# Block-causal attention with a gated convolution: the products of P and V in tiles of 64x64 instead of 64x32

## The chip, the cores and the metric

The kernel runs on one core of a Trainium2 chip. The metric is the device time of one execution in microseconds, the median of three runs. The matrix engine is called PE here (its weight loads PEld), the vector engine DVE, the scalar engine ACT, GpSimd POOL, and the engine that issues DMAs SP.

## The reference

Eight batches, eight heads, 576 positions, 64 channels a head. Attention is causal by blocks of 64 positions, and its output, heads side by side, goes through a layer with a convolution over positions and a gate:

```python
B, H, S, D = 8, 8, 576, 64
scores = matmul(q, k.transpose) / sqrt(D)
scores = where(block_i >= block_j, scores, -1e9)        # blocks of 64 positions
attn = exp(scores - max); attn = attn / (sum + 1e-9)
x = matmul(attn, v)                                     # then (B, S, H*D) = (8, 576, 512)
h = maximum(x @ w_in, 0)                                # w_in 512 x 1024
conv_out[s] = sum_k conv_w[k] * h[s + k - 1]            # three taps
out = (h * sigmoid(conv_out)) @ w_out                   # w_out 1024 x 512
```

## The kernel before

Work goes by pairs of heads: 32 pairs, four to a batch. The first batch's pairs are done in two parts, A (positions 0 to 255, blocks 0 to 3) and B (blocks 4 to 8); the 28 other pairs are done whole (blocks 0 to 8). Behind the last pair of a batch come its dense projections, `ffn` (L1005: x times w_in; L1071: the gated result times w_out), in float32r, with tiles of 128x128.

For a pair, `stage_s` makes the scores on PE (L862), in up to three sets of blocks: (8, 5), (7, 6) and (4, 3, 2, 1, 0). Each call takes 64 rows of the array (one head's 64 channels) and 32 columns (32 query positions): a tile of 64x32. DVE takes the maximum (L874), ACT the exponential with its sum (L890). `inverse` makes 1/sum on POOL and DVE, spread over a tile `rb`. `stage_pv` then

- transposes P in 32x32 pieces on DVE into `ptw` (or `pta` for part A), L939;
- multiplies by V on PE, L952, in `mm`. For each block u of keys it makes eight calls: y (two halves of the 64 channels), g (two halves of the 64 key and query rows) and h (two heads). V is the stationary operand, 64 rows by 32 columns; P moves, 32 query positions for every block that sees u, so 288 columns for u = 0 of a whole pair and 32 for u = 8. The results accumulate over u in two banks of PSUM, at partitions 64h + 32y, in bank g;
- multiplies the sum by `rb` on DVE (L963), rounds the high part on ACT (L967) and leaves the rest to POOL, for the projections.

A whole pair's P·V step has 9 x 8 = 72 calls. The step of part B has as many, with 160 columns for u = 0 to 4; that of part A has 4 x 8.

The order is written out by hand: the numbers in `ORDER` (L19) say in which sequence `Plan.follow` emits the operations recorded by `pl.op`, `BANKS` which PSUM bank each takes, and `FILLS` where spare matmuls stand (L1166). The durations given to `pl.op` do not set the order. One operation of the plan is one whole step of P·V; its calls stand one behind the other on PE.

Of the kernel before, what the change touches and what calls it, by code (L numbers as in the profile page):

```python
# [331 lines left out]
def kernel(  # L332
# [10 lines left out]
    nc = tc.nc  # L343
# [54 lines left out]
    def bank(tag):  # L398
        return pl.bank(psum, tag)

    def both(pair):
        a, b = sorted(x.slot for x in pair)
        assert b == a + 1
        return banks[:, a:b + 1]
# [35 lines left out]
    def held(tag, t, cap, before=None):  # L440
        b = Bin([])
        b.t = t[len(pl.tags.setdefault(tag, [])) % cap]
        hist = pl.tags[tag]
        hist.append(b)
        if len(hist) > cap:
            b.before = hist[-1 - cap]
        elif before is not None:
            b.before = before
        return b
# [14 lines left out]
    def c_act(n, psum=True, ap=False, acc=False):  # L464
        return (0.051 if psum else 0.093) + n / 1200.0 + (0.093 if ap else 0) + (0.08 if acc else 0)

    def c_dve(n, fast=False, two_in=False):
        return 0.065 + n / (1920.0 if fast else 960.0) + (0.05 if two_in else 0.0)

    def c_pool(n, two_in=False):  # L470
        return 0.145 + n * 0.0022 if two_in else 0.16 + n / 1200.0
# [348 lines left out]
    def c_tile(widths, more, least):  # L820
        return sum(max(2 * 0.000836 * w + more, least) for w in widths)
# [104 lines left out]
    def stage_pv(pq, done, vs, xx, at, part, ready):  # L926
        vat, vbufs, vdone = vs
        done, (rb, inv) = done
        b0, b1 = SPAN[part]
        if part == "A":  # L930
            pt = held("pta", pta, 2)
            rise, sl = 3, 0
        else:
            pt = held("ptw", [ptw], 1, firstp)
            rise, sl = RISE, 0
        ps = []
        for b, ns, t0 in done:
            def tr(b=b, x=pq[b], pt=pt):
                nc.vector.transpose(pt.ap[:, :, b:b + rise * b + 1:rise, :], x.ap.rearrange("p h (u n) -> p h u n", n=32))  # L939

            ps.append(pl.op(DVE, c_dve(64 * (b + 1)) + 0.025, tr, t0, deps=ns, bufs=[pq[b], pt] + ([firstp] if part == "A" else [])))
        vb = [bank("v"), bank("v")]

        def mm():
            for u in range(b1):
                lo = max(u, b0)
                for y in range(2):
                    for g in range(2):
                        for h in range(2):
                            r = slice(64 * g, 64 * g + 64)  # L950
                            o = 64 * h + 32 * y
                            nc.tensor.matmul(both(vb)[o:o + 32, g, 32 * (lo - b0):32 * (b1 - b0)].rearrange("p (b n) -> p b n", n=32),  # L952
                                             vat(u, h)[r, 32 * y:32 * y + 32], pt.ap[r, h, rise * u + lo:rise * u + b1, :],
                                             start=(u == 0), stop=(u == b1 - 1), skip_group_check=True)

        o = pl.op(PE, c_tile([32 * (b1 - max(u, b0)) for u in range(b1)], 0.03, 0.15), mm, at, deps=ps + vdone, bufs=vb + vbufs + [pt], area=0.85, rows64=3)
        w = 32 * (b1 - b0)

        def out(j):
            return xx[j].ap[:, 64 * b0:64 * b1].rearrange("p (b g n) -> p g b n", g=2, n=32)  # L960

        def mul():
            nc.vector.tensor_tensor(out=rb.ap[:, :, 0:b1 - b0, :], in0=both(vb)[:, :, 0:w].rearrange("p g (b n) -> p g b n", n=32),  # L963
                                    in1=rb.ap[:, :, 0:b1 - b0, :], op=ALU.mult)

        def evh():
            nc.scalar.activation(out=out(0), in_=rb.ap[:, :, 0:b1 - b0, :], func=AF.Copy)  # L967

        def evl():
            eng = nc.gpsimd if LOWPOOL else nc.vector  # L970
            eng.tensor_tensor(out=out(1), in0=rb.ap[:, :, 0:b1 - b0, :], in1=out(0), op=ALU.subtract)

        e = pl.op(DVE, c_dve(2 * w), mul, at + 3.0, deps=[o, inv], bufs=vb + [rb])
        e = pl.op(ACT, c_act(2 * w, False), evh, at + 3.5, deps=[e], bufs=[xx[0], rb])
        if LOWPOOL:
            es = [pl.op(POOL, c_pool(2 * w, True), evl, at + 4.0, deps=[e], bufs=[xx[0], xx[1], rb])]
        else:
            es = [pl.op(DVE, c_dve(2 * w, two_in=True), evl, at + 4.0, deps=[e], bufs=[xx[0], xx[1], rb])]
        ready(es)
# [141 lines left out]
    for i, (p, part) in enumerate(visits):  # L1121
        opv, ot = offs[part]
        b0 = base[i]
# [78 lines left out]
```

## Time and profile before

| what | value |
|---|---|
| time, median of 3 runs | 702.47 us (700.16 to 703.66) |
| the profiled execution: its time, its span | 701.78 us, 699.8 us |
| mean granted clock of PE | 0.995 of 2.4 GHz |
| PE, PEld busy | 665.2 us, 556.9 us |
| DVE, ACT, POOL busy | 574.9, 535.2, 325.3 us |
| L952 (P·V), PE busy | 93.0 us in the steps with `ptw` |
| L862 (scores), PE busy | 106.2 us |

The span runs from the first to the last instruction of the program. The chain of waits goes back from the last instruction to what released it, or to the instruction before on the same engine; "issue" in it, and as a releaser, is time in which the engine waited for nothing that the profile shows. A matmul's recorded duration holds its way through the array, so matmuls that follow each other overlap, and the steps between their starts say more than the durations.

### The profile page before, as it was taken

To read this page: it belongs to the slowest core of one execution; us is meant where nothing else is said; L and a number is where in the kernel's file an instruction comes from. 1 tells how busy PE (TensorE), PEld (TensorE's weight loads), DVE (VectorE), ACT (ScalarE), POOL (GpSimd) and SP (SyncE) were. 2 spreads that over 40 slices of the span, in tenths; PEclk is the share of its full clock that TensorE was granted. 3 is DMA by queue.
4 is the path that set the end of the run, shared out by engine and by line. 5 is a ranking of instruction groups with operands and counts; after the bars stand their busy time and mean duration, and the time that the engine had idled before them with its cause. 6 is when DMAs were issued, how large, how long until landed. Compare 5 with 4: busy or idle time off the path is not lost.

```text
span 699.8 us, 29716 instructions
## 1 busy us (share of the span) xinstructions
PE 665.2 (95%) x12059; PEld 556.9 (80%) x12059; DVE 574.9 (82%) x1345; ACT 535.2 (76%) x2000; POOL 325.3 (46%) x730
## 2 busy tenths in 40 slices
PE   9879989999999899999999999999999999999997
PEld 7556768878888688788888788787979787889986
DVE  4989989988997679897988779897989978986562
ACT  5877879967978667796988678977887768875663
POOL 2664545645545325436344444555436424444341
PEclk9999999999999999999999999999999999999999
DMA  7986653445255441416343443343343424130001
GB/s 169 213 175 132 127 114 50 94 95 88 46 108 92 78 86 39 81 42 128 76 78 68 84 99 59 61 105 58 73 95 62 93 64 96 27 68 1 35 27 61
DMA packets 238541, 58.58 MB, mean 84 GB/s; under 512 B 228524, under 2 KB 232900, under 8 KB 238404
## 3 DMA queue, kind: packets, MB, share of 16 engines
q1 hardware_dynamic: 237060, 55.76, 39.6%
q8 instruction: 95, 1.56, 1.0%
q10 hardware_dynamic: 1344, 0.92, 0.5%
q14 instruction: 42, 0.34, 0.2%
HBM read 47.21 MB, written 9.44 MB: 81 GB/s over the span
## 4 chain that ended last, share of the span: by engine, by line
PE 83%; ACT 6%; DVE 4%; issue 4%; DMA 1%; POOL 0%; ACTq 0%; DVEq 0%
PE banks L1005 27%; PE banks L1071 27%; PE banks L862 13%; PE banks L952 11%; ACT p L890 3%; PE banks L683 2%; PE banks L1166 1%; DVE st L874 1%; DMA gh<-in_moe_w_in_dram 1%; DVE ptw L939 1%; PE banks L680 1%; ACT t L1022 1%; DVE t L1030 1%; DVE t L1026 1%; DMA out_dram<-stage 1%
## 5 line engine op out<-in xcount | busy, mean ns | idle before, releaser
L890 ACT ACTIVATE p<-banks,st 128x128 f32<-128x128 f32 (+8 forms) x576 | 220.8, 398 | 19.7 <-DVE st L881 17.9
L1005 PE MATMUL banks<-x,wih 128*128 128x290 f32 (+3 forms) x1024 | 185.6, 300 | 1.0 <-issue 0.6
L1005 PEld LDWEIGHTS banks<-x,wih 128*128 128x128 f32 x1024 | 154.3, 189 | 10.9 <-issue 4.4
L498 POOL TENSOR_SCALAR st<-st 32x18 f32<-32x18 f32 (+4 forms) x344 | 85.1, 247 | 164.8 <-DVE st L874 93.1
L1045 POOL TENSOR_TENSOR gl<-t,gh 128x289 fp32r<-128x289 f32 (+3 forms) x128 | 106.4, 838 | 112.6 <-ACT gh L1042 98.4
L874 DVE TENSOR_REDUCE st<-banks 128x2 f32<-128x128 f32 (+8 forms) x288 | 125.8, 475 | 16.5 <-PE banks L862 14.4
L939 DVE STREAM_TRANSPOSE ptw<-p 128x128 f32<-128x128 f32 (+8 forms) x272 | 128.0, 497 | 13.4 <-ACT p L890 7.0
L890 ACT ACTIVATION_READ_ACCUMULATOR p<-banks,st 128x1 f32 x576 | 121.2, 210 | 0.0
L1071 PE MATMUL banks<-woh,gh 128*128 128x512 f32 (+1 forms) x296 | 119.9, 405 | 0.1
L862 PE MATMUL banks<-kT,qT 64*32 64x224 f32 (+8 forms) x4464 | 106.2, 302 | 13.4 <-issue 10.2
L1071 PE MATMUL banks<-wol,gh 128*128 128x512 f32 (+1 forms) x296 | 116.4, 393 | 0.0
L1071 PE MATMUL banks<-woh,gl 128*128 128x512 f32 (+1 forms) x296 | 116.3, 393 | 0.0
L862 PEld LDWEIGHTS banks<-kT,qT 64*32 64x32 f32 x4464 | 71.5, 105 | 41.8 <-issue 24.0
L1005 PE MATMUL banks<-x,wil 128*128 128x290 f32 (+3 forms) x512 | 104.8, 297 | 0.0
L952 PE MATMUL banks<-ptw,vn 64*32 64x96 f32 (+8 forms) x4608 | 93.0, 296 | 10.5 <-issue 9.8
L952 PEld LDWEIGHTS banks<-ptw,vn 64*32 64x32 f32 x4608 | 82.1, 105 | 24.8 <-issue 14.6
L1026 DVE SCALAR_TENSOR_TENSOR t<-h,cw,t 128x289 f32<-128x289 f32 (+3 forms) x128 | 69.4, 549 | 30.1 <-ACT t L1022 29.9
L1005 PEld LDWEIGHTS banks<-x,wil 128*128 128x128 f32 x512 | 81.4, 188 | 3.1 <-issue 1.3
L1030 DVE SCALAR_TENSOR_TENSOR t<-h,cw,t 128x287 f32<-128x287 f32 (+3 forms) x128 | 73.8, 585 | 1.6
L837 ACT ACTIVATE st<-st 32x4 f32<-32x4 f32 (+3 forms) x200 | 41.2, 207 | 44.3 <-DVE st L874 41.5
L1022 ACT ACTIVATE t<-h,cw 128x289 f32<-128x289 f32 (+3 forms) x128 | 67.5, 537 | 5.0 <-POOL gl L1045 1.8
L1035 ACT ACTIVATE t<-t 128x287 f32<-128x287 f32 (+3 forms) x128 | 55.9, 446 | 17.4 <-DVE t L1030 17.0
(93 smaller groups left out, 838.0 us busy)
## 6 DMA issues: line engine op xcount, KB each, us to landing
vn<-in_v_dram SPq DMA_DIRECT2D x128, 144.0 KB, 3.6
out_dram<-stage SPq DMA_DIRECT2D x35, 256.0 KB, 2.5
qT<-in_q_dram SPq DMA_DIRECT2D x112, 72.0 KB, 3.1
kT<-in_k_dram SPq DMA_DIRECT2D x112, 72.0 KB, 3.2
x<-in_moe_w_out_dram SPq DMA_DIRECT2D x8, 512.0 KB, 3.8
gl<-in_moe_w_in_dram SPq DMA_DIRECT2D x4, 512.0 KB, 5.8
vxa<-in_v_dram SPq DMA_DIRECT2D x8, 128.0 KB, 5.2
gh<-in_moe_w_in_dram SPq DMA_DIRECT2D x2, 512.0 KB, 5.4
```

The costliest lines, as they stand in the source:

```text
L498: nc.gpsimd.tensor_scalar(out=dst, in0=src, scalar1=1.0, scalar2=0.0, op0=ALU.mult, op1=ALU.add)
L862: nc.tensor.matmul(both(sb)[32 * quad:32 * quad + 32, h, o:o + w].rearrange("p (u n) -> p u n", n=32), t["q"].ap[r, 64 * b + 32 * g:64 * b ...
L874: nc.vector.tensor_reduce(out=st.ap[:, 0, c, :], in_=both(sb)[:, :, off:off + w], op=ALU.max, axis=AX.X, negate=True)
L890: nc.scalar.activation(out=pt.ap[:, h, :], in_=both(sb)[:, h, off:off + w], func=AF.Exp, bias=st.ap[:, 2, c, h:h + 1], accum_out=st.ap[:, ...
L939: nc.vector.transpose(pt.ap[:, :, b:b + rise * b + 1:rise, :], x.ap.rearrange("p h (u n) -> p h u n", n=32))
L952: nc.tensor.matmul(both(vb)[o:o + 32, g, 32 * (lo - b0):32 * (b1 - b0)].rearrange("p (b n) -> p b n", n=32), vat(u, h)[r, 32 * y:32 * y + ...
L1005: nc.tensor.matmul(fb.ap[:, 0:n2], wt[:, c, fs], xs[c][xi].ap[:, x0:x0 + n2], start=(n + c - c0 == 0), stop=(n + c - c0 == 3 * NCC - 1))
L1022: nc.scalar.activation(out=t.ap[:, 0:no], in_=hb.ap[:, own:own + no], func=AF.Copy, scale=cw[:, NFC + f:NFC + f + 1])
L1026: nc.vector.scalar_tensor_tensor(out=t.ap[:, i0:no], in0=hb.ap[:, own + i0 - 1:own + no - 1], scalar=cw[:, f:f + 1], in1=t.ap[:, i0:no], o ...
L1030: nc.vector.scalar_tensor_tensor(out=t.ap[:, 0:i1], in0=hb.ap[:, own + 1:own + 1 + i1], scalar=cw[:, 2 * NFC + f:2 * NFC + f + 1], in1=t.a ...
L1045: nc.gpsimd.tensor_tensor(out=gbuf[1].ap[:, f, carry:carry + no], in0=t.ap[:, 0:no], in1=gbuf[0].ap[:, f, carry:carry + no], op=ALU.subtract)
L1071: nc.tensor.matmul(fb.ap[:, 0:cut], gbuf[a].ap[:, f, cs], w[:, f, ds], start=(f == 0 and n == 0), stop=(f == NFC - 1 and n == 2))
```

## The change

The loop over y goes. Each call now takes all 64 channels of V as the stationary operand, a tile of 64x64, and writes 64 partitions of PSUM. What is computed, and where each sum ends up, stays.

```diff
         def mm():
             for u in range(b1):
                 lo = max(u, b0)
-                for y in range(2):
-                    for g in range(2):
-                        for h in range(2):
-                            r = slice(64 * g, 64 * g + 64)
-                            o = 64 * h + 32 * y
-                            nc.tensor.matmul(both(vb)[o:o + 32, g, 32 * (lo - b0):32 * (b1 - b0)].rearrange("p (b n) -> p b n", n=32),
-                                             vat(u, h)[r, 32 * y:32 * y + 32], pt.ap[r, h, rise * u + lo:rise * u + b1, :],
-                                             start=(u == 0), stop=(u == b1 - 1), skip_group_check=True)
+                for g in range(2):
+                    for h in range(2):
+                        r, o = slice(64 * g, 64 * g + 64), slice(64 * h, 64 * h + 64)
+                        nc.tensor.matmul(both(vb)[o, g, 32 * (lo - b0):32 * (b1 - b0)].rearrange("p (b n) -> p b n", n=32),
+                                         vat(u, h)[r, :], pt.ap[r, h, rise * u + lo:rise * u + b1, :],
+                                         start=(u == 0), stop=(u == b1 - 1), skip_group_check=True)
```

Lines behind it move up by two: L952 becomes L950, L1005 L1003, L1071 L1069. No operation changes its place. On PE, the step that runs at 291 us before stands between the last rows of a score set and the projections; a row gives the line, out and in, the shape that is written and how many such calls follow each other:

```order
L862 MATMUL banks<-kT,qT 32x32 x8
L952 MATMUL banks<-ptw,vn 32x288 x8
L952 MATMUL banks<-ptw,vn 32x256 x8
L952 MATMUL banks<-ptw,vn 32x224 x8
L952 MATMUL banks<-ptw,vn 32x192 x8
L952 MATMUL banks<-ptw,vn 32x160 x8
L952 MATMUL banks<-ptw,vn 32x128 x8
L952 MATMUL banks<-ptw,vn 32x96 x8
L952 MATMUL banks<-ptw,vn 32x64 x8
L952 MATMUL banks<-ptw,vn 32x32 x8
L1005 MATMUL banks<-x,wih 128x290 x2
```

The same place of the changed kernel:

```order
L862 MATMUL banks<-kT,qT 32x32 x8
L950 MATMUL banks<-ptw,vn 64x288 x4
L950 MATMUL banks<-ptw,vn 64x256 x4
L950 MATMUL banks<-ptw,vn 64x224 x4
L950 MATMUL banks<-ptw,vn 64x192 x4
L950 MATMUL banks<-ptw,vn 64x160 x4
L950 MATMUL banks<-ptw,vn 64x128 x4
L950 MATMUL banks<-ptw,vn 64x96 x4
L950 MATMUL banks<-ptw,vn 64x64 x4
L950 MATMUL banks<-ptw,vn 64x32 x4
L1003 MATMUL banks<-x,wih 128x290 x2
```

Half the calls stand there, each 64 partitions high; the neighbours are the same. At 208 us the step stands between the projections and the next pair's scores, here its last rows and the score set behind, before:

```order
L952 MATMUL banks<-ptw,vn 32x64 x8
L952 MATMUL banks<-ptw,vn 32x32 x8
L862 MATMUL banks<-kT,qT 32x160 x8
L862 MATMUL banks<-kT,qT 32x128 x8
L862 MATMUL banks<-kT,qT 32x96 x8
```

and after:

```order
L950 MATMUL banks<-ptw,vn 64x64 x4
L950 MATMUL banks<-ptw,vn 64x32 x4
L862 MATMUL banks<-kT,qT 32x160 x8
L862 MATMUL banks<-kT,qT 32x128 x8
L862 MATMUL banks<-kT,qT 32x96 x8
```

There a tile of 64x64 now stands beside one of 64x32 where both were 64x32. In the whole order 19 P·V steps follow directly on scores and 17 are followed by scores.

## Rows read from the trace of the kernel before

**Rows 1.** The page: busy time, share of the span and number of instructions of each engine; the chain that ended last by engine.

```profile
PE 665.2 (95%) x12059; PEld 556.9 (80%) x12059; DVE 574.9 (82%) x1345; ACT 535.2 (76%) x2000; POOL 325.3 (46%) x730
...
PE 83%; ACT 6%; DVE 4%; issue 4%; DMA 1%; POOL 0%; ACTq 0%; DVEq 0%
```

**Rows 2.** PE's waits over the whole run: who waited for whom, us in total, times, the longest.

```profile
PE banks L862 <- issue: 10.9, 14, 1.5
PE banks L952 <- issue: 9.8, 12, 1.9
PE banks L862 <- ACT t L1035: 2.1, 1, 2.1
```

**Rows 3.** The same from 120 to 640 us.

```profile
PE banks L862 <- issue: 7.9, 10, 1.5
PE banks L952 <- issue: 7.9, 11, 1.1
...
PE banks L1005 <- issue: 0.6, 1, 0.6
PE banks L1005 <- ACT h L1019: 0.4, 1, 0.4
PE banks L862 <- ACT p L890: 0.3, 1, 0.3
```

**Rows 4.** Stretches from the end of one idle gap of PE to the end of a later one: from:to, length, busy time and (number) of PE, PEld, DVE, ACT, POOL, the granted clock, the DMA engines' share and GB/s.

```profile
155.03:190.88 35.85, 34.64 (x764) 29.97 (x764) 31.89 (x75) 29.55 (x120) 17.27 (x40) 1.00 0.40 69
190.88:213.20 22.32, 21.05 (x382) 17.45 (x382) 19.42 (x46) 18.76 (x72) 11.24 (x24) 1.00 0.41 86
213.20:233.63 20.43, 18.34 (x381) 15.72 (x381) 17.32 (x43) 16.41 (x65) 8.79 (x21) 1.00 0.49 86
233.63:248.21 14.58, 13.83 (x256) 10.66 (x256) 9.49 (x24) 9.65 (x43) 5.91 (x17) 0.88 0.50 84
248.21:294.27 46.06, 44.41 (x764) 38.03 (x764) 37.28 (x88) 33.59 (x127) 20.06 (x45) 1.00 0.37 73
```

**Rows 5.** DMA queues: packets, MB, their time as a share of 16 engines' time. First the whole run, then 291.4 to 293.0 us.

```profile
q8 instruction: 95, 1.56, 1.0%
...
q8 instruction: 1, 0.02, 5.7%
```

**Rows 6.** Instructions in order of time, merged, around 291 us: start, length, engine, line, operation, out<-in, shape, number, idle time before and its releaser. PE first, then a row of PEld.

```profile
290.76 0.56 PE L862 MATMUL banks<-kT,qT 64*32 64x96 f32 x34
291.20 2.27 PE L952 MATMUL banks<-ptw,vn 64*32 64x288 f32 x83
294.27 0.92 PE L952 MATMUL banks<-ptw,vn 64*32 64x128 f32 x61 [0.80 <-issue]
295.12 0.53 PE L1005 MATMUL banks<-x,wih 128*128 128x290 f32 x2
...
291.17 2.06 PEld L952 LDWEIGHTS banks<-ptw,vn 64*32 64x32 f32 x84
```

**Rows 7.** The same view of PE from 207.4 to 213.6 us.

```profile
207.70 0.39 PE L1071 MATMUL banks<-wol,gh 128*128 128x512 f32 x1
207.93 0.40 PE L1071 MATMUL banks<-woh,gl 128*128 128x512 f32 x1
208.25 2.81 PE L952 MATMUL banks<-ptw,vn 64*32 64x288 f32 x142
210.87 0.34 PE L862 MATMUL banks<-kT,qT 64*32 64x160 f32 x2
...
213.20 0.37 PE L862 MATMUL banks<-kT,qT 64*32 64x64 f32 x21 [1.27 <-issue]
```

**Rows 8.** The same view around a step without a gap.

```profile
465.33 2.82 PE L952 MATMUL banks<-ptw,vn 64*32 64x288 f32 x144
468.09 0.50 PE L1071 MATMUL banks<-woh,gh 128*128 128x512 f32 x1
```

**Rows 9.** Groups by line, operation and shape: number, busy us, mean ns of one, idle us before them. The weight loads of P·V, its widest matmuls, and the weight loads of a projection.

```profile
L952 PEld LDWEIGHTS banks<-ptw,vn 64*32 64x32 f32 x4608 | 82.1, 105 | 24.8 <-issue 14.6 <-DVE st L906 1.0 <-DVE t L1038 0.4
L952 PEld LDWEIGHTS banks<-pta,vxa 64*32 64x32 f32 x256 | 3.4, 105 | 2.1 <-ACT wil L692 1.1 <-DVE rb L963 1.0
L952 PE MATMUL banks<-ptw,vn 64*32 64x288 f32 x448 | 20.9, 409 | 0.0
L1005 PEld LDWEIGHTS banks<-x,wih 128*128 128x128 f32 x1024 | 154.3, 189 | 10.9 <-issue 4.4 <-ACT h L1019 1.0 <-ACT p L890 0.3
```

**Rows 10.** PE's waits from 0 to 120 us, the "issue" ones.

```profile
PE banks L862 <- issue: 2.9, 4, 1.0
PE banks L952 <- issue: 1.9, 1, 1.9
```

**Rows 11.** Two stretches, columns as in rows 4.

```profile
50.00:120.00 70.00, 65.48 (x1154) 50.10 (x1153) 65.80 (x149) 57.19 (x187) 34.97 (x78) 0.98 0.56 113
120.00:640.00 520.00, 500.51 (x9793) 425.88 (x9793) 444.86 (x1037) 410.84 (x1593) 247.05 (x556) 1.00 0.39 76
```

**Rows 12.** PE in order of time behind the gap that ends at 409.06 us.

```profile
409.06 0.36 PE L952 MATMUL banks<-ptw,vn 64*32 64x64 f32 x19 [1.01 <-issue]
409.35 0.40 PE L1005 MATMUL banks<-x,wih 128*128 128x288 f32 x1
```

## The prediction

> **What bounds the kernel now.** I read the busy table first, then the chain, then TensorE's waits, then the places where it waits. PE is busy 95% of the span, the next engine, DVE, 82%; the chain that ends last lies 83% on PE, and 4% of it, 28 us, is "issue": time in which PE waited for nothing that the profile shows [rows 1]. So PE sets the time, and the reader should look at what PE does when it does nothing. Its idle gaps are 9.8 us in 12 places in the lines of P times V (L952) and 10.9 us in 14 places in those of the scores (L862), all "issue"; 2.1 us more are put down to an ACT [rows 2]. Real waits for other engines are small, and in the middle of the run (120 to 640 us) nearly absent: 0.4 and 0.3 us [rows 3].
>
> What ends such a gap can be read from counts. Between the ends of six gaps PE issued 764+764, 382+382, 381+381, 256+256 and 764+764 matmuls and weight loads [rows 4]: 6, 3, 3, 2 and 6 times 254 to 256. The queue named "instruction" made 95 transfers of 1.56 MB together, 16.4 KB each, and 24118 instructions over 95 is again 254 [rows 1, 5]. One such transfer lies inside 291.4 to 293.0 us, and the gap there ends at 294.27 [rows 5, 6]. So a gap is TensorE having run through a block of some 254 instructions before the next was there. The gap at 294.27 comes after 83 matmuls and 84 loads of its step, so its block began 87 instructions before 291.20, in the score rows that begin at 290.76, near 290.6 us [rows 6]: from there to 294.27 are 3.6 us. My estimate from that: a block that lasts under about 3.6 us stalls, a longer one does not. The dense projections pass 2 instructions in 0.23 us (207.70 to 207.93, rows 7), 254 in 29 us, and never stall long; a P·V step passes 288 in 2.76 us (465.33 to 468.09, rows 8), a score step follows as densely. The 231 us gap, put down to ACT, ends on such a count too (381+381), so I take it as one of them.
>
> The Trainium skill, "Runtime: NRT & Kernel Launch", section "Instruction fetch mechanics", speaks against this: blocks of 256 instructions are fetched while the last one runs, and crossing a boundary is "mostly hidden". By that the gaps would have another cause, and halving the instructions would give nothing there. The counts agree with its block and not with its "hidden"; it is a rival below.
>
> **The change part by part.** A call in float32 is two loads and two matmuls in the trace (a step of 72 calls shows x144, rows 8). L952 has 4608 + 256 loads and as many matmuls [rows 9]; both halve. PE's instructions fall from 24118 by 4864 to 19254, and the transfers from 95 to about 76. No row of the order moves and no wait is added.
>
> *Stalls.* A P·V step now passes 144 instructions in its 2.6 to 2.8 us, so a block that holds one needs 110 others: more than 3.6 us together with dense rows, about 3.5 us when they are scores. From 120 us on the gaps are 7.9 + 7.9 + 2.1 + 0.6 = 18.5 us in 23 places [rows 3]. One costs more than its idle time: the step at 291.20 hands over at 295.12, after 3.92 us, against 2.76 undisturbed, 1.16 lost for 0.80 shown [rows 6, 8]. I take +0.2 for each, between 0 and 0.36: 18.5 + 4.6 = 23.1 us (18.5 to 26.8). Before 120 us lie 2.9 + 1.9 = 4.8 us [rows 10], but there DVE is busy 65.8 of 70 us [rows 11], and PE waits for ACT and DVE anyway, so I count half, 2.4 (0 to 4.8). The gap at 231 us also left its mark on the clock: granted 0.88 over the 14.58 us behind it [rows 4], a part of them at the lower level of 1.2 GHz, which gives away 0.12 x 14.58 = 1.7 us; it goes with the gap. Left over: blocks that fall into a whole score step with the P·V step beside it. Such a pair has 160 + 144 instructions, so a boundary leaves a full block in it 50 times in 254; with some 17 such places that is three or four, at most 0.6 us each: 2 us (0 to 6).
>
> *Streaming.* The same columns pass with four tiles side by side instead of eight. Today 448 matmuls of 288 columns and 409 ns mean are 183 us of work in 20.9 us of busy time [rows 9], so the eight tiles do run together. No row shows 64x64 tiles. Bounds: nothing, if four run together; twice the columns if only two do, which is a rival. I take nothing, as the nearest row is the eight-tile one.
>
> *Weights.* A load takes 105 ns for 32 columns and 189 for 128 [rows 9], so an estimate for 64 is 133 ns; it lies behind the matmuls of the pass before except in the two narrowest widths, four passes, 0.11 us a step. Against that the narrow end is paced by the number of instructions: the last 19 matmuls behind the gap at 409.06 take 0.29 us [rows 12], 15 ns each, and of the last 32 half go: 0.24 us. Net -0.05 us for 36 steps, -2 us (-9 to +4).
>
> *Change of tile shape.* Scores keep 64x32 tiles, so P·V beside scores becomes a change of shape. The order shows 19 steps entered from scores and 17 left to them. From 64x32 to 128x128 the step at 465.33 takes 2.76 us, that at 208.25, which goes on to scores, 2.62 (to 210.87): 0.14. From 128x128 into 64x32 it is 0.32 us (207.93 to 208.25) where one matmul after another takes 0.23: 0.09 [rows 7, 8]. 36 x 0.11 = +4 us (0 to +5).
>
> The Trainium skill, "TensorEngine Tiling (Array Packing)", section "Key Properties", says that a change of tiling mode drains the engine. The two prices above agree, for changes to and from 128x128. By its rule the 4 us stand; without it the sum would be 4 us lower, near 676.
>
> *Who is late next.* DVE works 444.9 of the 520 us in the middle [rows 11], 86%; in about 500 it would be 89%, ACT 82%. Both also wait for PE now. I allow 1.5 us of new waits (0 to 6).
>
> Sum on the profiled execution: 701.8 (span 699.8 and 2.0 around it) - 23.1 - 2.4 - 1.7 + 2 - 2 + 4 + 1.5 = 680.1. The median of the runs is 0.7 above the profiled one, which leaves it at 680.
>
> **The rivals.**
> Slower: 64x64 tiles do not run four at a time. For it: no row shows them. Against: eight tiles of half the size do. At two at a time each step streams its columns twice, 2.76 - 0.14 - 0.24 (the shape change and the narrow end, above) = +2.4 us for each of the 28 whole steps, 78% of that for the four of the second half of batch 0 (1120 of 1440 columns) and 22% for the four of the first: 2.4 x 32 = +77 us, so 680 + 77 = 757. The change stops paying where the tiles stream 22/77 = 29% slower. The Trainium skill, same page, section "Available Configurations", lists 64x64 as four tiles; no run here shows it.
>
> Only P·V's own stalls go, and the scores, as dense as before, keep theirs: then 7.9 + 11 x 0.2 = 10.1 us and 1 us of the early ones are gained, +4 and -2 stay, +1: 694. For it: score rows stall as often as P·V rows. Against: the score stalls I followed stand right behind a P·V step (208.25, stall to 213.20, rows 7), in the same block.
>
> Loads and shape changes cost more: if no pass can be shorter than its load's 133 ns, the eight passes of the four narrow widths take at least 8 x 0.133 = 1.06 us; were they twice as fast now, that is 0.5 us lost a step, 36 x 0.5 = 18 us: 698 to 702. For it: nothing shows a 64-column load. Against: loads run side by side today, 4608 of 105 ns (484 us) in 82.1 us of busy time [rows 9].
>
> The gaps are not instruction transfers: nothing of the 27 us, +4 - 2: 704. The counts in rows 4 make this unlikely.
>
> That the change does not do what it says is excluded by the order: x4 with 64 columns stands wherever x8 with 32 stood.
>
> **How the numbers follow.** Forecast (668 to 690 us) 0.72; only P·V's stalls 0.13; loads dearer 0.05; other cause 0.03; tiles not together 0.07. About 0.5%, 3.5 us, is what a measurement of this kernel tells from no change. Faster than 699 are the first two and half of the third: 0.88; within 0.5% the rest of the third and half of the fourth: 0.04; slower 0.08. The range takes the forecast's own and the second case: 668 to 695.
>
> **What would show it.** 9627 matmuls and about 76 transfers of the instruction queue; "issue" in P·V near 0 and in the scores 2 us or less; P·V steps of 2.5 to 2.8 us with x72; loads near 133 ns; the granted clock at 1.00 throughout 120 to 640. It would be wrong if the steps grow beyond 3 us, if "issue" in the scores stays near 8 us, or if PE's waits for DVE and ACT rise by several us.

## The result and the profile after

| | before | after |
|---|---|---|
| time, median of 4 runs | 702.96 us (700.16 to 703.66) | 677.68 us (676.38 to 678.41) |
| the profiled execution: its time, its span | 701.78, 699.8 us | 676.38, 674.4 us |
| PE busy, and the rest of its span | 665.2, 34.6 us | 657.6, 16.8 us |

The ratio is 0.965, with a 95% interval of 0.961 to 0.968: 25 us faster. The forecast was 680 us, in a range of 668 to 695.

The page of the changed kernel: busy time of each engine, the queue of instructions, and the chain that ended last, by engine.

```profile
PE 657.6 (98%) x9627; PEld 543.1 (81%) x9627; DVE 575.1 (85%) x1345; ACT 534.4 (79%) x2000; POOL 325.4 (48%) x730
...
q8 instruction: 76, 1.25, 0.8%
...
PE 26%; DVE 10%; ACT 7%; issue 2%; POOL 1%; DMA 1%; SPq 1%; DVEq 0%; ACTq 0%; POOLq 0%
```

PE's 9627 matmuls and as many loads came in 76 transfers, against 12059 and 95 [rows 1, 5]. The view could follow this chain back to 351 us only, so its shares add to half of the span. Within the followed half PE has 26 of 48 parts, and DVE and ACT together 17: the chain is no longer one of PE alone.

PE's waits over the whole run, the six largest: who waited for whom, us in total, times, the longest.

```profile
PE banks L862 <- ACT p L890: 1.5, 5, 0.6
PE banks L686 <- DVE wol L619: 1.4, 1, 1.4
PE banks L680 <- ACT woh L664: 1.3, 2, 0.9
PE banks L1164 <- DVE wol L492: 1.1, 1, 1.1
PE banks L1003 <- DVE rb L961: 0.9, 2, 0.7
PE banks L950 <- ACT wil L692: 0.8, 1, 0.8
```

Where "issue" led that list with 10.9 and 9.8 us [rows 2], no row of it is left, in any line; the view counts gaps from 0.15 us on. What remains are real waits, each small. The middle of the run in one window: PE is busy 496 of 500 us, at the full clock.

```profile
120.00:620.00 500.00, 496.00 (x7660) 416.59 (x7652) 442.55 (x1025) 407.74 (x1582) 246.89 (x551) 1.00 0.40 78
```

Two P·V steps in order of time, the one before projections that had its gap at 291 us before [rows 6], and one before scores.

```profile
277.35 2.71 PE L950 MATMUL banks<-ptw,vn 64*64 64x288 f32 x72
279.99 0.53 PE L1003 MATMUL banks<-x,wih 128*128 128x290 f32 x2
...
296.07 2.71 PE L950 MATMUL banks<-ptw,vn 64*64 64x288 f32 x72
298.71 1.64 PE L862 MATMUL banks<-kT,qT 64*32 64x288 f32 x53
```

Each hands over after 2.64 us, in one row without a break. Four tiles of 64x64 pass the columns as fast as eight of 64x32 did (2.62 and 2.76 us, rows 7, 8).

Where the 25.4 us of the profiled span went is worked out from the starts of all matmuls, each counted until the next one starts. P·V takes 88.3 us where it took 102.2, the scores 103.3 where they took 116.8, the projections and the preparation 2.5 us more than before; the other 0.6 us lie behind the last matmul. So half of the gain, 13.5 us, lies in the scores, where no instruction was changed. By time: the step that starts at 122.73 us before starts at 118.00, and the last step, at 635.16 before, at 610.44; so 4.7 us were won by then and 20.0 between the two.

### The profile page after: what moved, and what is told of

Read it like the earlier page. It is cut to its first block, busy times and chain, and to the rows that moved or that the text cites. A ratio compares the mean times of both kernels' runs of the same rounds, so it can differ in the third digit from the quotient of the medians.

```text
span 674.4 us, 24852 instructions
## 1 busy us (share of the span) xinstructions
PE 657.6 (98%) x9627; PEld 543.1 (81%) x9627; DVE 575.1 (85%) x1345; ACT 534.4 (79%) x2000; POOL 325.4 (48%) x730
## 5 line engine op out<-in xcount | busy, mean ns | idle before, releaser
L1003 PE MATMUL banks<-x,wih 128*128 128x290 f32 (+3 forms) x1024 | 186.2, 300 | 1.5 <-DVE rb L961 0.9
L1003 PEld LDWEIGHTS banks<-x,wih 128*128 128x128 f32 x1024 | 153.5, 188 | 12.8 <-issue 3.7
L1069 PE MATMUL banks<-woh,gh 128*128 128x512 f32 (+1 forms) x296 | 118.9, 402 | 0.4 <-ACT h L1017 0.2
L1069 PE MATMUL banks<-woh,gl 128*128 128x512 f32 (+1 forms) x296 | 115.5, 390 | 0.1
L1069 PE MATMUL banks<-wol,gh 128*128 128x512 f32 (+1 forms) x296 | 115.2, 389 | 0.0
L862 PE MATMUL banks<-kT,qT 64*32 64x224 f32 (+8 forms) x4464 | 102.9, 302 | 3.2 <-ACT p L890 1.5
L1003 PE MATMUL banks<-x,wil 128*128 128x290 f32 (+3 forms) x512 | 104.7, 297 | 0.0
L862 PEld LDWEIGHTS banks<-kT,qT 64*32 64x32 f32 x4464 | 70.1, 105 | 30.7 <-issue 5.8
L950 PEld LDWEIGHTS banks<-ptw,vn 64*64 64x64 f32 x2304 | 72.1, 133 | 19.2 <-issue 3.1
L950 PE MATMUL banks<-ptw,vn 64*64 64x160 f32 (+8 forms) x2304 | 85.4, 297 | 0.6 <-DVE st L906 0.6
L1003 PEld LDWEIGHTS banks<-x,wil 128*128 128x128 f32 x512 | 81.5, 188 | 3.1 <-issue 1.3
```

Of the source, the lines that this page charges most:

```text
L862: nc.tensor.matmul(both(sb)[32 * quad:32 * quad + 32, h, o:o + w].rearrange("p (u n) -> p u n", n=32), t["q"].ap[r, 64 * b + 32 * g:64 * b ...
L950: nc.tensor.matmul(both(vb)[o, g, 32 * (lo - b0):32 * (b1 - b0)].rearrange("p (b n) -> p b n", n=32), vat(u, h)[r, :], pt.ap[r, h, rise * ...
L1003: nc.tensor.matmul(fb.ap[:, 0:n2], wt[:, c, fs], xs[c][xi].ap[:, x0:x0 + n2], start=(n + c - c0 == 0), stop=(n + c - c0 == 3 * NCC - 1))
L1069: nc.tensor.matmul(fb.ap[:, 0:cut], gbuf[a].ap[:, f, cs], w[:, f, ds], start=(f == 0 and n == 0), stop=(f == NFC - 1 and n == 2))
```

## The experiments

The theory: PE stalled because its instructions came too late, and the change pays by being shorter to issue. The rivals: 64x64 tiles stream better in themselves (tile theory); the gaps had another cause; the fetch of instructions is no limit.

**The same tiles, with the instructions put back.** In the changed kernel, calls of 96 columns or more are made as two of half the columns, 256 instructions for a whole step instead of 144. Both halves of the first call of a sum carry the flag that begins it; the output is not the layer's, and only the times are used.

```diff
-                        nc.tensor.matmul(... lo:b1 ...)
+                        half = (lo + b1) // 2
+                        for x0, x1 in (((lo, half), (half, b1)) if b1 - lo > 2 else ((lo, b1),)):
+                            nc.tensor.matmul(... x0:x1 ...)
```

> 64x64 tiles as in the change, but every P·V call over 96 columns or more is made as two calls of half the columns: the same columns pass, the tile shapes are those of the change, and the step of a whole pair has 256 instructions instead of 144 (288 before the change). If the gain is the shorter instruction stream (instruction transfers that come too late), the gaps come back in P·V and in the scores, 11 to 18 us of issue in both together, each about 1 us, and the time is 686 to 697 us. If the gain is in the tiles of 64x64 themselves or in the narrow end of the step, nothing comes back: 676 to 680 us, no issue above 1 us.

Measured: 689.66 us (689.05 to 689.78, 4 runs), ratio 0.983 (0.979 to 0.987). PE's waits for "issue", which are two rows of the whole run, and the step that stands where 277.35 stood:

```profile
PE banks L952 <- issue: 4.4, 7, 1.6
PE banks L862 <- issue: 2.8, 6, 0.6
```

```profile
284.15 2.60 PE L952 MATMUL banks<-ptw,vn 64*64 64x128 f32 x100
287.43 0.68 PE L952 MATMUL banks<-ptw,vn 64*64 64x32 f32 x28 [0.69 <-issue]
288.04 0.53 PE L1005 MATMUL banks<-x,wih 128*128 128x290 f32 x2
```

The gaps are back in 64x64 tiles, so the shape of the tile doesn't prevent them, and half of the gain is gone. Their sum, 7.2 us, is less than the 11 to 18 expected. Another part of the loss is no gap: with 64 calls instead of 36 an undisturbed step takes 2.90 us (304.08 to 306.98) instead of 2.64, and 32 x 0.26 is 8 us. Gaps and longer steps together are 15 us, more than the 12 us lost; by starts, the projections give 4 us of it back.

**Few instructions in the old tiles.** Two attempts, both in the kernel before. The first made only one half of the channels for each block of keys but the first, in turn the lower and the upper one; the other half's sums are left out.

```diff
-                for y in range(2):
+                for y in range(2) if u == 0 else (u % 2,):
```

> Tiles of 64x32 as before the change, but behind the first block of keys each block multiplies only one half of the channels (even blocks the lower, odd blocks the upper): the output lacks those products. A whole pair's step has 160 instructions, nearly as few as the change's 144; the columns that pass are the same, and no change of tile shape stands between P·V and scores. If the number of instructions is the cause, issue falls under 2 us as in the change, and the time is below the change's 677.7 by what 36 changes of shape cost, 674 us (4 us on PE, some of it taken up by other engines). If the 64x64 tiles are the cause, the time stays near 702, at least above 690.

Measured: 674.17 us (673.25 to 674.72, 4 runs), ratio 0.961 (0.958 to 0.964). It doesn't tell the theories apart, since it took streaming time out of the step as well:

```profile
295.96 1.83 PE L952 MATMUL banks<-ptw,vn 64*32 64x288 f32 x80
297.81 1.01 PE L862 MATMUL banks<-kT,qT 64*32 64x288 f32 x28
```

A step takes 1.85 us, not 2.64: neighbouring blocks use different tiles and run side by side. The second attempt keeps to one half, so that the columns pass one behind the other in the same four tiles:

```diff
-                for y in range(2):
+                for y in range(2) if u == 0 else (0,):
```

> Tiles of 64x32 as before the change; behind the first block of keys only the lower half of the channels is multiplied, always the same one, so that the blocks follow each other in the same four tiles (in e2 they alternated between two sets of tiles and ran side by side, which took the step of a whole pair to about 1.85 us). The upper half of the output lacks those products. 160 instructions a step; no change of tile shape between P·V and scores. If the number of instructions is the cause, no issue is left and a step takes 2.5 to 2.7 us; the 36 changes of shape are then the only thing that the change pays and this kernel does not, 0.1 us each: 674 us (673 to 676) if PE still sets the time, 676 to 678 if other engines take up what PE gains. If the tiles of 64x64 are the cause of the gain, 690 us or more.

Measured: 675.16 us (675.09 to 676.83, 4 runs), ratio 0.964 (0.960 to 0.969), where the change has 0.965.

```profile
278.39 2.65 PE L952 MATMUL banks<-ptw,vn 64*32 64x288 f32 x80
280.97 0.40 PE L1005 MATMUL banks<-x,wih 128*128 128x290 f32 x1
```

```profile
PE banks L862 <- ACT p L890: 2.8, 6, 0.8
PE banks L686 <- DVE wol L619: 1.4, 1, 1.4
...
PE banks L862 <- issue: 0.6, 1, 0.6
```

The steps last about as long as those of the change (2.58 us here), the instructions are about as few (9915 matmuls), "issue" is one gap of 0.6 us, and the time is the change's, in 64x32 tiles. The tile theory falls.

The first attempt serves for something else. It shows what more relief of PE would be worth: its P·V takes 68.9 us in all (by starts, as above), 19.4 less than the change's, yet the span of its profiled execution is only 1.6 us shorter (672.8 against 674.4), the median of its runs 3.5. Its waits tell where the rest stays:

```profile
PE banks L862 <- ACT p L890: 11.4, 20, 1.6
PE banks L862 <- DVE rb L963: 5.8, 8, 1.2
```

PE now waits for the exponentials and for the scaling by 1/sum: these two rows hold 17.2 us, where the same rows of the change hold 1.8.

**Half of the change.** In the kernel before, every second step of P·V takes 64x64 tiles, the others keep the old ones. Both kinds stand in one run, among the same neighbours.

```diff
+        turns.append(part)
+        wide = len(turns) % 2 == 0
...
+                for y in range(1 if wide else 2):
...
+                            z = 64 if wide else 32
```

> Every second P·V step has the change's calls of 64x64 (18 of 36), the others those of before. If an instruction transfer that comes too late is the cause, gaps stand only in steps of x144 and in scores beside them, none in a step of x72; issue is 6 to 14 us instead of 23 and the time lies near the middle, 685 to 695 us. If the step's own streaming were the gain, it would be half of it as well, but the gaps would stay where they are.

Measured: 687.03 us (684.89 to 688.19, 4 runs), ratio 0.981 (0.976 to 0.987): half of the gain. The time alone could be half of any cause; the places of the gaps decide. "Issue" is 11.6 us in 13 places over the whole run, 6.8 us in 9 places from 120 to 620 us, the first two rows here. Then two steps of each kind, and what stands behind the old ones:

```profile
PE banks L862 <- issue: 5.2, 6, 1.5
PE banks L957 <- issue: 1.6, 3, 0.6
```

```profile
183.54 2.79 PE L957 MATMUL banks<-ptw,vn 64*32 64x288 f32 x142
186.16 0.21 PE L957 MATMUL banks<-ptw,vn 64*32 64x32 f32 x2
187.38 1.12 PE L862 MATMUL banks<-kT,qT 64*32 64x160 f32 x69 [0.71 <-issue]
205.25 2.71 PE L957 MATMUL banks<-ptw,vn 64*64 64x288 f32 x72
...
510.84 2.71 PE L957 MATMUL banks<-ptw,vn 64*64 64x288 f32 x72
525.20 2.46 PE L957 MATMUL banks<-ptw,vn 64*32 64x288 f32 x97
528.22 0.71 PE L957 MATMUL banks<-ptw,vn 64*32 64x96 f32 x47 [0.56 <-issue]
```

All nine gaps from 120 us on stand inside a step of 144 (three) or in the scores next behind one (six), none at a step of 72. The scores' own instructions are the same behind both, so their gaps come from the step before them.

**The gaps moved by a count.** In the kernel before, the first three stretches of spare matmuls are made of twice as many calls with half the columns: the same columns, 58 instructions more, all ahead of the P·V steps from 30 us on.

```diff
-                nc.tensor.matmul(... [P, 4, P] ...)
...
+                for c in (0, 2) if early else (0,):
+                    w = 2 if early else 4
+                    nc.tensor.matmul(... [P, w, P] ...)
```

> The kernel before the change, with its first 29 spare matmuls of 512 columns (all in the first 20 us) made as 58 of 256: the same columns, 58 instructions more ahead of everything else. If the gaps stand at the borders of transferred blocks, each border falls on an instruction 58 earlier in the program: the gap in the P·V step near 291 us comes after 54 or 55 matmuls instead of 83, and counts of instructions between gaps are multiples of 254 to 256 again; the time is 697 to 707, as gaps come and go by where the borders fall. If the gaps are waits for data, that gap stays behind 83 matmuls.

Measured: 697.94 us (695.67 to 700.08, 10 runs), ratio 0.995 (0.993 to 0.997). One step of the kernel before:

```profile
405.38 2.68 PE L952 MATMUL banks<-ptw,vn 64*32 64x288 f32 x125
```

Behind that row stands the gap of 1.01 us that ends at 409.06 [rows 12]. The same step here:

```profile
406.77 2.35 PE L952 MATMUL banks<-ptw,vn 64*32 64x288 f32 x96
409.99 0.72 PE L952 MATMUL banks<-ptw,vn 64*32 64x96 f32 x48 [0.87 <-issue]
```

The gap moved from behind matmul 125 to behind 96: 29 matmuls with their loads, 58 instructions earlier, to the instruction. Work and waits of this step are what they were, so a cause by count is shown. The gap named for the step near 291 us came in its place but not in its size: the view shows that step unbroken (x144), in 3.22 us instead of 2.76, and by the starts of its matmuls a pause of 0.31 us stands behind matmul 54, as expected.

The traces hold the same proof without an edit. PE's queue has 24118 loads and matmuls before the change and 159 entries for semaphores and drains, 24277 in all: 94.8 blocks of 256, for 95 transfers. Numbered in order, each matmul behind its load, all 27 gaps of "issue" and the one put down to ACT t L1035 end at entry 193 or 194 of such a block, and none of PE's other waits there does. In the runs of this section all 60 gaps of "issue" stand at these two entries as well.

One gap grew out of all proportion:

```profile
PE banks L862 <- issue: 16.0, 14, 5.2
PE banks L952 <- issue: 4.1, 7, 1.1
```

The 5.2 us stand from 37.6 to 42.8 us, a stretch in which all DMA engines are busy with data (share 1.08, columns as in rows 4); the block's transfer began there at 39.5 us, 2 us after PE had run out. Why it began so late stays open.

**The cost of a block by itself.** Behind the changed kernel's last work stand 512 calls in float32 of 32 columns, in eight tiles of 64x32, 2048 instructions with little to stream.

```diff
+    for i in range(64):
+        for quad in range(4):
+            for g in range(2):
+                nc.tensor.matmul(banks[32 * quad:32 * quad + 32, g, 0:32], ...)
```

> The changed kernel with 512 more float32 calls of 32 columns in eight tiles of 64x32 behind the last output (2048 instructions that wait for nothing; their result is not used). If a block of instructions takes about 3.6 us to come, PE runs 127 or 128 matmuls, stands still, and so on: one block every 3.4 to 4.2 us, 27 to 34 us in all, time 705 to 712. If PE's own issue is the limit (15 ns a matmul), it runs through without gaps: 15 to 17 us, time 692 to 695.

Measured: 701.87 us in one run, 24 above the change's median. PE's rows there:

```profile
670.84 2.29 PE L1174 MATMUL banks<-woh 64*32 64x32 f32 x248
675.64 1.29 PE L1174 MATMUL banks<-woh 64*32 64x32 f32 x128 [2.52 <-issue]
679.12 1.55 PE L1174 MATMUL banks<-woh 64*32 64x32 f32 x128 [2.18 <-issue]
683.13 1.55 PE L1174 MATMUL banks<-woh 64*32 64x32 f32 x128 [2.47 <-issue]
687.15 1.55 PE L1174 MATMUL banks<-woh 64*32 64x32 f32 x128 [2.47 <-issue]
```

PE goes in bursts of 128 matmuls and 128 loads, 256 instructions, each 1.3 to 1.6 us long, and one burst starts every 3.5 to 4.0 us (675.64, 679.12, 683.13, 687.15). That is the block and its price, in calls that wait for nobody. The trace has the transfers too: from the second burst on, each starts about 1.1 us after a burst has begun, takes 1.0 to 1.5 us, and the next burst begins 1.3 to 1.6 us after its end. So one block is fetched while the one before it runs. A limit of PE's own in issuing would have spread the calls evenly; that rival falls. The first burst is longer, 248 pairs: the running block and the next were there when the dense part began. In all it lasts 29 us (670.84 to the end of the span at 699.9), within the 27 to 34 expected. The time grew by less, 24 us, since the 3.5 us that stood behind the change's last matmul now pass beside it.

## Why the prediction was right, point by point

*The bound.* "A gap is TensorE having run through a block of some 254 instructions before the next was there": shown. The block has 256 (dense calls), the gaps move with the count (58 instructions) and sit only where the instructions are dense (every other step). The transfers agree: at 294.27 PE goes on 1.3 us after the end, at 292.97, of the one in rows 5, and behind the 21 longest stalls from 120 us on it does so after 1.3 to 1.7 us. The Trainium skill, "Runtime: NRT & Kernel Launch", section "Instruction fetch mechanics", has the blocks right; that crossing one is "mostly hidden" holds here, behind 120 us, for blocks that last over 4 us, and not for the denser ones.

*Stalls.* From 120 us on 23.1 us were expected and 2.0 left over; no "issue" is left. The half of the early gaps was too little: 4.7 us were won by the step at 122.73, as much as all the early gaps hold (4.8, rows 10) and not the 2.4 taken, although DVE is as busy there as before (67.5 of 70 us). Some of it may be clock, which the sum left out there: 0.98 was granted from 50 to 120 us [rows 11], and 1.00 now.

*The left-over.* Here a size was off. The 3.6 us below which a block stalls came from one place. I have since counted on in blocks of 256 from where the gaps end, and taken each block's time and the pause at its end from the starts of matmuls. Before, 21 blocks behind 120 us end in a pause of 0.6 us or more; they passed in 1.5 to 2.8 us, and block and pause together come to 2.9 to 3.8. In the changed kernel nine blocks behind 120 us pass in under 4 us, in 2.2 to 3.7, more than the three or four I had, and none ends in a pause over 0.33 us. So the term was 0 instead of 2. A bound by length alone can't say why, since 2.2 us now passes without a stall. What differs there is when the transfer starts: for the block at 221.41, which passes in 2.2 us, it began 0.1 us before the block did, for the 21 stalled ones 0.2 to 1.4 us behind their start.

*Streaming and weights.* 64x64 tiles run four at a time (2.64 us a step), and a load takes the 133 ns estimated:

```profile
L950 PEld LDWEIGHTS banks<-ptw,vn 64*64 64x64 f32 x2304 | 72.1, 133 | 19.2 <-issue 3.1 <-DVE st L906 1.3 <-DVE t L1024 1.1
```

The "issue" of the load row is idle time of the loading side and none of PE's: no matmul waits so. The rival of two tiles at a time (757 us) and that of dear loads (698 to 702) are out.

*Change of tile shape.* A step into 128x128 went from 2.76 to 2.64 us, so the narrow end and the loads give 0.12. The prediction's own two figures give as much, 0.24 less 0.11; its net of 0.05 was added up wrongly, and the term should have been -4.7 us, not -2. A step into scores would then be 2.50 and takes 2.64: 0.14 for the change of shape, as estimated. On the way in, the last matmul of a score set is followed by P·V later than before (starts): by 0.08 us in five places, after 0.12 us instead of 0.04, and by 0.13 to 0.15 in nine, against 0.09 estimated. The rule of the Trainium skill, "TensorEngine Tiling (Array Packing)", section "Key Properties", that such a change drains the engine, agrees with this price, now for 64x64 beside 64x32 as well.

*The clock.* It is 1.00 from 120 to 620 us, where 0.88 stood in one stretch [rows 4]; the 1.7 us went with the gap.

*Who is late next.* PE's waits for others from 120 to 620 us come to 3.6 us, by the rows of that window, against 0.7 [rows 3]: 2.9 us of new waits for 1.5 taken.

*The sum.* The profiled execution (676.4) beat the 680.1 worked out for it by 3.7 us. With the narrow end added up rightly the forecast for it would have been 677.4. (For the median the prediction adds 0.7 to its 680.1, which makes 680.8 and not 680.) The early gaps (2.3) and the left-over (2.0) came out better than taken, the new waits 1.4 us worse, which makes 674.5 of the 677.4; the 1.9 us that remain, on the other side, I don't assign to one term. So the mechanism and the large term are right, and that the total came as near as it did is partly luck: small errors cancel.

*Only P·V's own stalls go* (694 us, a chance of 0.13): out, since the scores won 13.5 us.

## What to carry to other kernels

"Issue" in TensorE's waits is worth counting: where the numbers of matmuls and loads between the ends of two gaps are multiples of one block, the engine runs out of instructions, and calls that do more each are worth more than their streaming shows, the neighbours included. A call in float32 counts as four instructions (72 calls of a step stand as x144 loads and x144 matmuls). Once those gaps are gone, look at the next engines before making the matmuls shorter still: here 19.4 us less of P·V gave 2 to 4 us.

## What the runs showed of the hardware

A dense run of matmuls and loads gets one block of 256 instructions every 3.5 to 4.0 us, of which the transfer itself takes 1.0 to 1.5. In the one run that shows it, the first 496 instructions of the dense run, which stood behind projections, passed without a stall. When a transfer comes isn't fixed: one that was needed while all DMA engines were busy with data cost PE 5.2 us. And the same columns take longer in more calls even with no gap: 2.90 against 2.64 us a step for 256 against 144 instructions.
